# Attention and a mish MLP on one core: the copy of the softmax factors for GpSimd moves behind VectorE's own three tiles

## The chip, the cores and the metric

The kernel runs on one core of a Trainium2 chip. The metric is the device time of the core in microseconds (us), given as the median of several executions. Before the change it is 480.37 us (three runs, 480.23 to 481.23).

The engines are named as in the profile: PE is TensorE (PEld its weight loads), DVE is VectorE, ACT is ScalarE, POOL is GpSimd, SP is SyncE, which here only issues DMAs.

## The reference

The program has two parts. The first is attention for 8 batches of 12 heads, 448 tokens, 64 channels, with a softmax whose denominator has one term more than usual:

```python
scores = scale * np.matmul(q, k.transpose(0, 1, 3, 2))
m = np.max(scores, axis=-1, keepdims=True)
e = np.exp(scores - m)
attn = e / (np.sum(e, axis=-1, keepdims=True) + np.exp(-m) + 1e-09)
return np.matmul(attn, v).astype(np.float32)
```

Its output, as 3584 rows of 768, goes through an MLP with a mish-like activation:

```python
h = x @ w_in                      # 768 -> 2048
sp = np.where(h > 20.0, h, np.log1p(np.exp(np.minimum(h, 20.0))))
g = h * np.tanh(sp)
return (g @ w_out).astype(np.float32)   # 2048 -> 768
```

All inputs and the output are float32; the kernel computes its matmuls in bfloat16.

## The kernel before

**Tiling.** Heads are worked on in pairs: 8 batches of 6 pairs are 48 pairs, numbered p = 0 to 47. A pair has 2 x 448 = 896 query rows, which are 7 tiles of 128 rows (NTILE = 7). For each tile the scores against all 448 keys lie in PSUM, and the exponentials go to a buffer `en` in SBUF (128 rows, 4 groups of keys, 7 tiles, 112 keys of a group). There are four `en` buffers, used in turn.

**One pair.** The pair's q and k are loaded by SP (`load_pair`, L132), cast to bfloat16 on GpSimd (`cast_pair`, L175 and L176, v in `cast_v`, L162), transposed on TensorE (L193) and copied out of PSUM (`evac_qk`, L212 to L235). `scores` makes the score matmuls in four steps (L266 to L289) and a maximum on DVE (L293); `exps` makes the exponentials and their sums on ACT (L306), and one more exponential for the added term of the denominator (L313). `denominators` adds the terms and takes the reciprocal on DVE (`rden`, L319 and L323). `normalise` multiplies each of the seven tiles of `en` by its row's factor. Then `en` must be turned, so that keys lie on the partitions: by a DMA transpose from SP (L345), or tile by tile on TensorE (`turn_on_pe`, L356, seven transposes to a group of keys, copied out of PSUM by DVE in L360). The turned tile `eT` is multiplied with v on TensorE (`av_pair`, L382), and the result is copied to `xT` (L391).

**Stages.** The first six pairs, those of batch 0, form the head: attention alone, pair after pair, four steps to a pair, since no MLP work exists yet. After the scores of pair p have begun, the pair before it is normalised. From pair 6 on the pairs come in units of three: in a unit the attention of a batch is interleaved with the MLP's two matmuls of earlier batches (`mm1_mish`, L406, its activation in L412; `mm2_part`, L472). The first matmul of the MLP starts at 63.40 us.

**Order of the work.** The order is written out by hand: the kernel is recorded under a manual schedule, and each engine carries out its instructions in the order in which the Python code issues them. The framework only adds the waits between engines. Each engine and each DMA queue is thus a line in which work stands behind what was issued before it. On GpSimd the casts of a later pair stand behind the tiles that it normalises; on SP the loads of later pairs stand behind the DMA transposes.

**Who normalises.** In the head, for the pairs 0 to 5, `normalise` is called with `shared=BY_POOL`, and BY_POOL is 4 (L564 and L573): GpSimd takes the tiles 0 to 3, DVE the tiles 4 to 6. In the later units, two pairs of three are done by DVE alone (L635 and L644), and one by GpSimd alone (`on_pool=True`, L646). Whenever GpSimd takes part, DVE first copies the seven factors per row from `rden` to a tile of their own, `rden2` (L331), which GpSimd's instructions read (L339); DVE's read `rden` (L341).

**How the pairs of the head are turned.** BY_PE (L518) names the pairs 2, 4, 5, 6 and 7 as those turned on TensorE; the pairs 0, 1 and 3 of the head go by DMA transpose. TURN_HEAD (L524) places the four groups of pair 2 in steps 2 and 3 of pair 3 and steps 0 and 1 of pair 4, and the first two groups of pair 4 in steps 2 and 3 of pair 5. AV_HEAD (L528) places the AV products of the pairs 0, 2 and 1 in the pairs 3 and 4. A group of L356 reads its seven tiles in order, so tiles of GpSimd's come first; each of the seven weight loads of a pair's first group waits for its own tile.

Of the kernel before, what the change touches and what calls it, by code (L numbers as in the profile page):

```python
# [9 lines left out]
FP32 = mybir.dt.float32  # L10
BF16 = mybir.dt.bfloat16
AF = mybir.ActivationFunctionType
ALU = mybir.AluOpType
# [6 lines left out]
def kernel(  # L20
# [9 lines left out]
    nc = tc.nc  # L30
# [6 lines left out]
    SP_ = S // NT  # L37
# [3 lines left out]
    NTILE = 2 * S // 128  # L41
# [11 lines left out]
    def pool(name, bufs, space=None):  # L53
        if space is None:
            return ctx.enter_context(tc.tile_pool(name=name, bufs=bufs))
        return ctx.enter_context(tc.tile_pool(name=name, bufs=bufs, space=space))
# [6 lines left out]
    st_pool = pool("st", 5)  # L63
# [261 lines left out]
    def normalise(p, dma=True, on_pool=False, shared=0):  # L325
        st = att[p]
        en = st["en"]
        if on_pool or shared:

            st["rden2"] = st_pool.tile([128, NTILE], FP32, tag="rden2", name="rden2")  # L330
            nc.vector.tensor_copy(out=st["rden2"], in_=st["rden"])  # L331
        for i in range(NTILE):
            pool_does = on_pool or i < shared
            args = dict(
                out=en[:, :, i, 0:SP_], in0=en[:, :, i, 0:SP_],
                scalar1=st["rden2" if pool_does else "rden"][:, i : i + 1],
            )
            if pool_does:
                nc.gpsimd.tensor_scalar(scalar2=1.0, op0=ALU.mult, op1=ALU.mult, **args)  # L339
            else:  # L340
                nc.vector.tensor_scalar(scalar2=None, op0=ALU.mult, **args)  # L341
        eT = eT_pool.tile([128, NT, 2 * S], BF16, tag="eT", name="eT")
        st["eT"] = eT
        if dma:
            nc.sync.dma_start_transpose(  # L345
                out=eT.rearrange("c j (i q) -> c (j i) q", q=128),
                in_=en.rearrange("q j i c -> q (j i c)"),
            )
# [199 lines left out]
    for p in range(HEAD):  # L548
        for s in range(STEPS):
            if s == 1 and p == 0:  # L550
                transpose_pair(p + 2)
            exps(p * STEPS + s)
            if p == 0 and s == 0:
                evac_qk(1, act=True)
            if s == 1:
                evac_qk(p + 2, act=True)
            flush_late()
            scores_ahead(HEAD * STEPS + 3)
            if s == (2 if p == HEAD - 1 else 0):
                load_pair(p + 4)  # L560
            if s == 0:
                if p:
                    denominators(att[p - 1])
                    normalise(p - 1, dma=p - 1 not in BY_PE, shared=BY_POOL)  # L564
                    transpose_pair(p + 2)
                cast_pair(p + 3)
                load_w(W_HEAD.get(p, 0))
            for part in TURN_HEAD.get((p, s), []):
                turn_on_pe(*part)
            if (p, s) in AV_HEAD:  # L570
                av_pair(AV_HEAD[p, s], act=True)
    denominators(att[HEAD - 1])
    normalise(HEAD - 1, dma=HEAD - 1 not in BY_PE, shared=BY_POOL)  # L573

    for u in range(UNITS_PER_B, N_UNITS + 2 * UNITS_PER_B):
# [50 lines left out]
        for f in range(FF_U):  # L626
            if moe:
                mm1_mish(b, w * FF_U + f)
            if u == UNITS_PER_B and f in (2, 6):
                load_w(1)  # L630
            if not attn:
                continue
            if f == 0:
                denominators(att[p0]["whole"])
                normalise(todo[0], dma=todo[0] not in BY_PE)  # L635
            if f in (1, 3, 5):
                transpose_pair(nxt + f // 2, bank=f // 2 % 2)
                evac_qk(nxt + f // 2)
            if nxt < DIAG_FROM and f in (4, 6):
                scores_ahead(nxt * STEPS + f // 2 - 1)  # L640
            if f == FF_U - 1:
                scores_ahead(min(nxt * STEPS + 3, N_PAIRS * STEPS))
            if f == 3:
                normalise(todo[1], dma=todo[1] not in BY_PE)  # L644
            if f == 4:
                normalise(todo[2], dma=todo[2] not in BY_PE, on_pool=True)  # L646
# [37 lines left out]
```

## Time and profile before

| what | value |
|---|---|
| median of three runs | 480.37 us (480.23 to 481.23) |
| the profiled execution: time | 479.95 us |
| the profiled execution: span from first to last instruction | 478.0 us |
| TensorE busy | 443.1 us (93%) |
| ACT busy | 350.0 us (73%) |
| DVE busy | 339.1 us (71%) |
| GpSimd busy | 181.1 us (38%) |
| copies of factors (L331) | 20, about 0.165 us each |
| DVE tiles (L341) | 214, median 0.330 us |
| GpSimd tiles (L339) | 122, median 0.641 us |

The profiled execution is one execution; its own time stands beside the span, and sums are made against it. A line of a group names the source line, the engine, the operation, output and input with their shapes, the count, then the busy time, the mean duration in ns, and the idle time of the engine just before with what ended it. A line of a timeline names the start, the duration of the whole merged group, the engine and the line. Instructions of DVE and ACT overlap a little at their ends, so that start to start is less than the duration. The chain that ended last lists, in order of time, the pieces of work in which each released the next.

### The profile page before, as it was taken

The numbers are of one execution on the slowest core, as the hardware profiler recorded it, in microseconds if no ns is written. First come the engines' busy times: TensorE is split into PE (matmuls) and PEld (weight loads), VectorE is DVE, ScalarE is ACT, GpSimd is POOL, SyncE is SP. The second block draws the span as 40 slices with busy tenths as digits, with TensorE's granted clock in tenths as the row PEclk, the third lists the DMA queues.
The fourth block names the chain that finished last, engine by engine and source line by source line (L and its number), as shares of the span: only waits on it lengthen the run. The fifth ranks groups of instructions, "written<-read, shape, count | busy, mean of one in ns | idle before, by whom it ended". The sixth has DMA issues, their size and how long they took to land.

```text
span 478.0 us, 8924 instructions
## 1 busy us (share of the span) xinstructions
PE 443.1 (93%) x3064; PEld 248.6 (52%) x3064; DVE 339.1 (71%) x680; ACT 350.0 (73%) x919; POOL 181.1 (38%) x315
## 2 busy tenths in 40 slices
PE   4565888898999999999999999999999999999997
PEld 2233544454655555555555555556555555556565
DVE  4888987968787886878687878788787869420021
ACT  5979678878787888979787878888897978412300
POOL 4877809255514334353535242433535340300000
PEclk9998798899999999999999999999999999999999
DMA  8999969999999989899999999899989595870113
GB/s 228 220 233 220 235 100 234 162 187 238 207 217 276 206 212 219 213 203 246 193 250 182 225 167 228 211 207 234 201 233 212 156 178 127 135 164 24 43 28 105
DMA packets 202381, 90.37 MB, mean 189 GB/s; under 512 B 159072, under 2 KB 198880, under 8 KB 202336
## 3 DMA queue, kind: packets, MB, share of 16 engines
q1 hardware_dynamic: 194848, 83.51, 81.3%
q0 software_dynamic: 7488, 6.29, 8.6%
q8 instruction: 24, 0.39, 0.3%
q14 instruction: 21, 0.17, 0.1%
HBM read 45.61 MB, written 11.01 MB: 118 GB/s over the span
## 4 chain that ended last, share of the span: by engine, by line
PE 76%; ACT 10%; DVE 9%; issue 2%; DMA 1%; POOL 0%; SPq 0%; DVEq 0%; ACTq 0%; POOLq 0%
PE mo L472 26%; PE mo L406 25%; ACT en L306 9%; PE sc L382 6%; DVE negm L293 6%; PE sc L266 5%; PE sc L406 4%; PE sc L193 3%; PE sc L272 2%; PE mo L356 1%; PE mo L382 1%; DVE en L341 1%; PE sc L280 1%; DVE eT L360 1%; DMA k_f<-in_k_dram 1%
## 5 line engine op out<-in xcount | busy, mean ns | idle before, releaser
L306 ACT ACTIVATE en<-sc,negm 128x448 bf16<-128x448 f32 x336 | 209.6, 637 | 26.4 <-DVE xT L391 10.4
L293 DVE TENSOR_REDUCE negm<-sc 128x2 f32<-128x896 f32 x192 | 180.7, 968 | 55.8 <-PE sc L275 26.0
L472 PE MATMUL mo<-w_out_sb,gT 128*128 128x384 bf16 (+1 forms) x912 | 142.3, 301 | 0.0
L406 PE MATMUL mo<-xT,w_in_sb 128*128 128x448 bf16 x672 | 137.7, 353 | 0.6 <-DVE xT L391 0.6
L412 ACT ACTIVATE gT<-mo 128x448 bf16<-128x448 f32 x112 | 61.3, 547 | 68.2 <-PE mo L406 68.1
L472 PEld LDWEIGHTS <-gT 128*128 128x128 bf16 x912 | 84.1, 98 | 48.2 <-issue 5.7
L339 POOL TENSOR_SCALAR en<-en,rden 128x448 bf16<-128x448 bf16 x122 | 76.4, 646 | 80.7 <-DVE rden L331 76.9
L406 PEld LDWEIGHTS <-w_in_sb 128*128 128x128 bf16 x768 | 72.9, 98 | 64.0 <-issue 3.0
L306 ACT ACTIVATION_READ_ACCUMULATOR en<-sc,negm 128x1 f32 x336 | 69.3, 206 | 0.0
L175 POOL CAST q_bf<-q_f 112x512 bf16<-112x512 f32 x47 | 29.0, 617 | 98.4 <-DMA q_f<-in_q_dram 98.0
L341 DVE TENSOR_SCALAR en<-en,rden 128x448 bf16<-128x448 bf16 x214 | 58.6, 345 | 0.9
L459 DVE COPY o_sb<-mo 128x384 f32<-128x384 f32 (+1 forms) x65 | 32.2, 495 | 35.1 <-PE mo L472 34.8
L266 PE MATMUL sc<-kT,qd 128*128 128x448 bf16 x168 | 47.7, 354 | 0.3 <-ACT en L306 0.2
L272 PE MATMUL sc<-kT,qd 64*128 64x448 bf16 x72 | 25.1, 411 | 12.7 <-ACT en L306 11.1
L382 PE MATMUL sc<-eT,v_bf 112*64 112x448 bf16 x288 | 34.1, 357 | 1.9 <-ACT en L306 1.7
L162 POOL CAST v_bf<-v_f 112x512 bf16<-112x512 f32 x48 | 29.5, 616 | 9.7 <-DMA v_f<-in_v_dram 8.8
L382 PEld LDWEIGHTS <-v_bf 112*64 112x64 bf16 x384 | 21.0, 112 | 22.8 <-issue 13.6
L176 POOL CAST k_bf<-k_f 112x512 bf16<-112x512 f32 x47 | 28.9, 616 | 7.5 <-DMA k_f<-in_k_dram 7.0
L227 DVE TENSOR_SCALAR qd<-sc 64x448 bf16<-64x448 bf16 x48 | 18.7, 389 | 11.9 <-PE sc L193 11.2
L266 PEld LDWEIGHTS <-qd 128*128 128x128 bf16 x168 | 16.3, 97 | 18.0 <-issue 9.2
L275 PE MATMUL sc<-kT,qd 64*128 64x448 bf16 x72 | 25.4, 415 | 0.0
L472 PE MATMUL mo<-w_out_sb,mid 128*128 128x384 bf16 x128 | 24.9, 326 | 0.0
(57 smaller groups left out, 340.1 us busy)
## 6 DMA issues: line engine op xcount, KB each, us to landing
q_f<-in_q_dram SPq DMA_DIRECT2D x48, 224.0 KB, 5.1
k_f<-in_k_dram SPq DMA_DIRECT2D x48, 224.0 KB, 5.4
v_f<-in_v_dram SPq DMA_DIRECT2D x48, 224.0 KB, 5.7
w_in_sb<-in_moe_w_in_dram POOLq DMA_DIRECT2D x12, 256.0 KB, 6.1
w_out_sb<-in_moe_w_out_dram POOLq DMA_DIRECT2D x8, 384.0 KB, 7.6
out_dram<-o_sb SPq DMA_DIRECT2D x7, 336.0 KB, 3.3
out_dram<-o_sb SPq DMA_DIRECT2D x8, 288.0 KB, 4.6
out_dram<-o_sb SPq DMA_DIRECT2D x8, 240.0 KB, 2.9
```

The source lines that it names most:

```text
L162: nc.gpsimd.tensor_copy(out=casted[p][2], in_=loaded.pop(p)[2])
L266: nc.tensor.matmul(sc[:, bk, 0:S], lhsT=qT[:, i].rearrange("d h r -> d (h r)"), rhs=kT, start=True, stop=True,)
L272: nc.tensor.matmul(sc[:, 0, 0:S], lhsT=qT[0:64, qa : qa + 128], rhs=kA, start=True, stop=True)
L293: nc.vector.tensor_reduce(out=negm, in_=sc[:, 0 : len(cols), 0:S], axis=AX.X, op=ALU.max, negate=True)
L306: nc.scalar.activation(out=st["en"][:, :, c, 0:SP_], in_=sc[:, bk, 0:S].rearrange("q (j c) -> q j c", j=NT), func=AF.Exp, bias=st["negm"][ ...
L339: nc.gpsimd.tensor_scalar(scalar2=1.0, op0=ALU.mult, op1=ALU.mult, **args)
L341: nc.vector.tensor_scalar(scalar2=None, op0=ALU.mult, **args)
L382: nc.tensor.matmul(av[h * 64 : (h + 1) * 64, 0:S], lhsT=v_bf[:, h, j * D : (j + 1) * D], rhs=e_h, start=(j == 0), stop=(j == NT - 1),)
L406: nc.tensor.matmul(h_ps[:, 0:S], lhsT=w_in_sb[:, dm, ff * 128 : (ff + 1) * 128], rhs=xT[b][:, dm, :], start=(dm == 0), stop=(dm == DM_T - 1),)
L412: nc.scalar.activation(out=gT[b][:, ff, :], in_=h_ps[:, 0:S], func=AF.Mish)
L459: nc.vector.tensor_copy(out=o_sb[:, cols], in_=st["o"][:, 0:n_cols])
L472: nc.tensor.matmul(st["o"][:, 0:n_cols], lhsT=src[:, ff, c0 : c0 + 128], rhs=w_out_sb[:, ff, cols], start=(ff == 0), stop=(ff == FF_T - 1),)
```

## The change

In `normalise` the loop over all seven tiles is split. DVE's tiles, from `n_pool` to 6, now come first; after them, if GpSimd has tiles, DVE copies the factors, and GpSimd's tiles follow. Where GpSimd does a whole pair, DVE has no tile of that pair, so its order does not change; where DVE does a whole pair there is no copy. The order on DVE thus changes in the pairs 0 to 5 alone: three tiles and then the copy, in place of the copy and then three tiles. The order on the other engines and on the DMA queues is the same. In the changed file the lines from there on have numbers larger by two (L356 becomes L358, L382 becomes L384, and so on); DVE's tiles become L335, the copy L339, GpSimd's tiles L341.

```diff
-        if on_pool or shared:
-
-            st["rden2"] = st_pool.tile([128, NTILE], FP32, tag="rden2", name="rden2")
-            nc.vector.tensor_copy(out=st["rden2"], in_=st["rden"])
-        for i in range(NTILE):
-            pool_does = on_pool or i < shared
-            args = dict(
-                out=en[:, :, i, 0:SP_], in0=en[:, :, i, 0:SP_],
-                scalar1=st["rden2" if pool_does else "rden"][:, i : i + 1],
-            )
-            if pool_does:
-                nc.gpsimd.tensor_scalar(scalar2=1.0, op0=ALU.mult, op1=ALU.mult, **args)
-            else:
-                nc.vector.tensor_scalar(scalar2=None, op0=ALU.mult, **args)
+        n_pool = NTILE if on_pool else shared
+
+        def scaled(i, rden):
+            tile_i = en[:, :, i, 0:SP_]
+            return dict(out=tile_i, in0=tile_i, scalar1=rden[:, i : i + 1])
+
+        for i in range(n_pool, NTILE):
+            nc.vector.tensor_scalar(scalar2=None, op0=ALU.mult, **scaled(i, st["rden"]))
+        if n_pool:
+
+            rden2 = st_pool.tile([128, NTILE], FP32, tag="rden2", name="rden2")
+            nc.vector.tensor_copy(out=rden2, in_=st["rden"])
+            for i in range(n_pool):
+                nc.gpsimd.tensor_scalar(
+                    scalar2=1.0, op0=ALU.mult, op1=ALU.mult, **scaled(i, rden2)
+                )
```

## The prediction

> **What bounds the kernel now.** I read the page's busy times and slices first, then the chain that ended last, then the timeline around the six pairs that the change touches, then which waits the late work would meet.
>
> The page's busy times, the slices of the granted clock, and the two groups at stake:
>
> ```profile
> PE 443.1 (93%) x3064; PEld 248.6 (52%) x3064; DVE 339.1 (71%) x680; ACT 350.0 (73%) x919; POOL 181.1 (38%) x315
> ...
> PEclk9998798899999999999999999999999999999999
> ...
> L339 POOL TENSOR_SCALAR en<-en,rden 128x448 bf16<-128x448 bf16 x122 | 76.4, 646 | 80.7 <-DVE rden L331 76.9
> ...
> L341 DVE TENSOR_SCALAR en<-en,rden 128x448 bf16<-128x448 bf16 x214 | 58.6, 345 | 0.9
> ```
>
> From 63 us on TensorE hardly stops, so whatever the first 63 us (the head) lose reaches the end in full. The change touches only pairs 0 to 5, normalised between 17 and 54 us. The chain of waits there, around pair 2:
>
> ```profile
> 28.54 0.21 DVE rden L323
> 28.75 0.02 issue
> 28.77 0.17 DVE rden L331
> ...
> 30.90 0.53 PE sc L272
> 31.42 0.03 PE sc L275
> 31.45 0.98 PE mo L356 x7
> 32.44 0.48 PE sc L272
> ```
>
> TensorE turns pair 2 (L356) on the path itself; four of its seven tiles are GpSimd's. The timeline of the normalising, pair 0 (17 us) and pair 2 (28 us):
>
> ```profile
> 17.28 0.17 DVE L331 COPY rden<-rden 128x7 f32<-128x7 f32 x1
> 17.36 0.82 DVE L341 TENSOR_SCALAR en<-en,rden 128x448 bf16<-128x448 bf16 x3
> 18.10 1.08 DVE L293 TENSOR_REDUCE negm<-sc 128x2 f32<-128x896 f32 x1
> ...
> 28.85 1.13 DVE L341 TENSOR_SCALAR en<-en,rden 128x448 bf16<-128x448 bf16 x3
> 29.90 1.07 DVE L293 TENSOR_REDUCE negm<-sc 128x2 f32<-128x896 f32 x1
> ...
> 29.11 2.60 POOL L339 TENSOR_SCALAR en<-en,rden 128x448 bf16<-128x448 bf16 x4 [1.47 <-DVE rden L331]
> 31.66 0.61 POOL L175 CAST q_bf<-q_f 112x512 bf16<-112x512 f32 x1
> ```
>
> Three DVE tiles take 0.82 us in pair 0, where GpSimd's first tile took 0.96 beside them, and 1.13 in pair 2, where the third DVE tile alone took 0.64 and GpSimd's first 0.74. So one of the two engines pays some 0.3 us where they overlap.
>
> Last, busy time and granted clock in stretches of 3.41 us (columns: stretch, length, then busy time of PE, PEld, DVE, ACT, POOL, then the clock):
>
> ```profile
> 30.88:34.29 3.41, 3.39 (x22) 2.16 (x23) 2.82 (x5) 1.91 (x7) 3.21 (x6) 1.00 1.14 255
> 34.29:37.70 3.41, 2.25 (x28) 1.41 (x25) 2.68 (x9) 2.69 (x8) 1.00 (x2) 1.00 0.97 210
> 41.12:44.53 3.41, 1.47 (x16) 0.80 (x13) 2.49 (x8) 3.41 (x12) 1.40 (x2) 1.00 1.20 216
> 47.94:51.36 3.42, 2.75 (x20) 1.82 (x20) 3.28 (x10) 2.41 (x8) 1.69 (x4) 0.50 1.08 264
> 51.36:54.77 3.41, 3.41 (x20) 1.43 (x19) 3.41 (x6) 2.06 (x6) 3.41 (x7) 0.50 1.13 247
> 78.67:82.08 3.41, 3.29 (x25) 2.25 (x22) 3.25 (x5) 3.36 (x12) 3.41 (x7) 0.50 1.04 234
> ```
>
> The clock changed at about 44.53 (down), 54.77 (up), 78.67 (down) and 82.08 (up): steps of 3, 7 and 1 times 3.41 us. Before 34.3 us the column says 1.00, yet the same matmul took 0.53 us at 30.90 and 0.35 at 36.83, so it rose at 34.29 too, on the same grid. It rose after stretches with TensorE busy 3.39, 3.41 and 3.29 us, and not after 2.75.
>
> **The change part by part.** Nothing is added or removed. In six pairs a 7-wide copy (0.17 us) moves on DVE behind three tiles. SP, ACT and GpSimd keep their order.
>
> *GpSimd starts later.* DVE's tiles start every 0.247 us where nothing disturbs them ((18.10 - 17.36) / 3), so the copy starts 0.74 later. GpSimd follows a copy's start by 0.34 to 0.37, as now. Its four tiles lose their contended start: the last three of pair 2 start every 0.61, so four take 2.44 instead of the 2.55 from 29.11 to 31.66. In pair 2: copy 29.51, first tile 29.85, last tile done near 32.30, not 31.71: 0.59 later. For pairs 1, 3, 4, 5 about the same, for pair 0 only 0.4, as its first tile takes 0.6 instead of 0.96.
>
> *DVE is free earlier.* Next operation at 29.51 + 0.08 = 29.59 instead of 29.90: 0.31 sooner in pairs 1 to 5, nothing in pair 0. In pairs 0 to 3 this is worth nothing: ACT's exps run without a gap over it (no idle between 28.64 and 32.8), and they set the pace.
>
> *Pair 2.* TensorE's weight loads of L356 follow at 0.1 us; the fourth was held until 31.76, 0.05 after GpSimd's last tile. There is no slack, so the whole 0.59 is a stall: the next scores, transposes, and the AV of pair 0 whose result ACT awaits (idle 2.21 us before 35.01) slip by it. Price 0.59; bounds 0.45 (the delayed copy with GpSimd regaining all of 0.3) and 0.74 (regaining nothing).
>
> *Pair 4.* L356 at 46.30; its fourth load came at about 46.62 with GpSimd done at 46.44. Now GpSimd is done 0.63 later, the load at 47.12: TensorE slips 0.5. DVE, busy until 47.48 anyway, slips 0.37. It then wins 0.31 back in pair 5, where it is the path (the eT copy at 50.63 releases L356 at 51.29). Net +0.06; bounds -0.31 and +0.5.
>
> *Pairs 0, 1, 3 and 5.* The DMA transposes of 0, 1 and 3 follow GpSimd's last tile or queue behind each other on SP: 0.4 to 0.6 later. They land in 8.3 to 9.6 us, so by about 30.1, 37.0 and, with both delays, 50.7; their readers run at 33.8, 40.4 and 60.3. The loads behind them on SP move as much as the casts that read them. Pair 5's turning starts at 54.76, GpSimd is done at about 53.4. The casts queued behind GpSimd's tiles finish k for the next pair at 21.98 and 27.73, 0.14 ahead of their loads into TensorE (22.12, 27.87): covered, narrowly. Weight loads issued by GpSimd at 55.74 and 58.18 feed matmuls after 91 us.
>
> *The clock.* With 0.59 us of stall the first stretch holds 3.39 - 0.59 = 2.80 us of work: nearest to the row with 2.75, after which the clock stayed down. Then it rises at 37.70, and the rest of the AV (0.66 warm), L286 (0.30), the transposes of the next pair (0.51) run cold: TensorE +1.5, of which ACT's queued exps hide about 1; ACT's qd starts near 37.8 instead of 36.66, 1.14 late, so 0.55 over the stall. Bounds: 0, if 2.80 is enough, and 1.6, if two later stretches are missed as well (51.36 and its next, 0.55 each). I take 0.55. [...]
>
> *Sum:* 0.59 + 0.06 + 0.55 = 1.20 on the profiled execution's 479.95 (span 478.0 and 1.95 around it): 481.15. That execution lies 0.42 under the median of 480.37; if runs of before differ in when their clock rises, some already pay part of the 0.55, and from the median I add 0.65 and about 0.2: 481.2. Both agree; the forecast is 481.2 us, +0.17%.
>
> **The rivals.**
> *Faster: DVE was the path.* If DVE's 0.31 counted in all of pairs 1 to 5, 1.55 us would go: 478.8. For it: the chain shows DVE's tiles at 28.94, and pair 5 does gain. Against: ACT has no gap there, and pair 2's stall stands in any case. It decides if GpSimd's last tile comes no later than now, which needs its tiles in 0.46 us each; the quickest here follow each other at 0.58. [...]
> *The clock is missed more widely.* Two later stretches too: 479.95 + 0.65 + 1.6 = 482.2. For it: any shift moves gaps across a fixed grid. Against: a gap may as well move out.
> *No clock effect:* 0.65 alone, 480.6 to 481.0.
> *Casts late.* If GpSimd needs 0.15 more per pair, k is late in two pairs and passes to ACT's qd, up to 0.4 each: 482.0.
> *The delay is hidden* (the order of DVE does change, but the fourth load has slack I don't see): 480.0 to 480.4.
>
> **How the numbers follow.** About 0.2% (1 us) is what a measurement can tell from no change. Forecast with one missed stretch 0.40 (480.8 to 481.7, half on each side of +0.2%, 481.33); no clock effect 0.20; clock missed more widely 0.20; casts late 0.06; hidden 0.05; faster 0.09. Slower 0.20 + 0.20 + 0.06 = 0.46, same 0.20 + 0.20 + 0.05 = 0.45, faster 0.09. The range reaches from 480.1 to 482.5: it leaves out the faster case and the ends of the others.
>
> **What would show it.** GpSimd's tiles after a gap-free 0.74 us of DVE tiles; four tiles in 2.44; a gap of about 0.6 inside the first L356 group of pair 2; L382 behind it at cold durations (eight in 1.7 instead of 1.18); ACT idle 2.8 or more before pair 0's xT; first MoE matmul about 1.2 after 63.40. Wrong if that group has no gap, or if the head ends no later.

## The result, and the profile after

The changed kernel takes 482.03 us, the median of twelve runs (480.89 to 483.26), beside 480.24 us for the kernel before (twelve runs, 479.11 to 482.86). The ratio is 1.0036, 95% interval 1.002 to 1.0052: slower by 0.96 to 2.5 us. A second measurement gave 481.89 beside 480.64 us, ratio 1.001, interval 0.9988 to 1.0031, which by itself does not exclude that nothing changed. (The ratios here and below are those on record; they can differ from the quotient of the two medians, which is 1.0026 in this case.) Together: slower, by somewhere near 0.2 to 0.3%, and the two intervals share 1.002 to 1.0031.

The profiled execution of the changed kernel took 482.24 us, with a span of 480.4 us; before it was 479.95 and 478.0. Its page, the lines that answer to those shown of before:

```profile
PE 445.3 (93%) x3064; PEld 249.5 (52%) x3064; DVE 337.4 (70%) x680; ACT 349.6 (73%) x919; POOL 179.4 (37%) x315
...
L341 POOL TENSOR_SCALAR en<-en,rden 128x448 bf16<-128x448 bf16 x122 | 75.3, 635 | 83.2 <-DVE rden L339 74.9
...
L335 DVE TENSOR_SCALAR en<-en,rden 128x448 bf16<-128x448 bf16 x214 | 57.1, 338 | 1.1
```

DVE is busy 1.7 us less than before (339.1 to 337.4) and GpSimd 1.7 us less (181.1 to 179.4): the two no longer meet at the start of a pair's normalising. TensorE is busy 2.2 us more (443.1 to 445.3) with the same 3064 matmuls. The engines that gained are not those that set the end.

Pair 2 in the timeline of the changed kernel, first DVE and GpSimd:

```profile
28.68 0.83 DVE L335 TENSOR_SCALAR en<-en,rden 128x448 bf16<-128x448 bf16 x3
29.42 0.16 DVE L339 COPY rden<-rden 128x7 f32<-128x7 f32 x1
29.50 1.08 DVE L293 TENSOR_REDUCE negm<-sc 128x2 f32<-128x896 f32 x1
...
29.75 2.48 POOL L341 TENSOR_SCALAR en<-en,rden 128x448 bf16<-128x448 bf16 x4 [1.46 <-DVE rden L339]
32.18 0.61 POOL L175 CAST q_bf<-q_f 112x512 bf16<-112x512 f32 x1
```

DVE's three tiles take 0.83 us instead of 1.13, and DVE goes on with the maxima at 29.50 instead of 29.90. GpSimd starts at 29.75 instead of 29.11 and its four tiles take 2.48 instead of 2.60. Then TensorE, which turns the pair, before and after:

```profile
31.39 1.05 PE L356 MATMUL mo<-ident,en 128*112 128x128 bf16 x7
...
33.78 1.18 PE L382 MATMUL mo<-eT,v_bf 112*64 112x448 bf16 x8
```

```profile
30.79 0.53 PE L272 MATMUL sc<-kT,qd 64*128 64x448 bf16 x1 [1.87 <-ACT en L306]
...
31.28 0.75 PE L358 MATMUL mo<-ident,en 128*112 128x128 bf16 x3
32.29 0.68 PE L358 MATMUL mo<-ident,en 128*112 128x128 bf16 x4 [0.26 <-POOL en L341]
...
34.30 1.70 PE L384 MATMUL mo<-eT,v_bf 112*64 112x448 bf16 x8
```

Before, the seven transposes ran without a gap from 31.39. Now the group breaks after three of them, and the fourth starts at 32.29, when GpSimd's fourth tile is done. The product behind it takes 1.70 us instead of 1.18, because the clock had not risen yet. The chain of waits around the same place answers to the chain shown of before (start, duration, engine, tile, line; some pieces left out). It is from a second profile of the changed kernel, as the chain of the first is not followed back so far:

```profile
28.81 0.32 DVE en L335
...
29.64 0.09 DVE rden L339
...
29.89 0.94 POOL en L341 x2
...
31.11 0.43 POOL en L341
...
31.73 0.65 POOL en L341
...
32.42 0.67 PE mo L358 x4
```

Before, the chain went from DVE's tiles over a maximum and ACT's exponentials to TensorE's scores. It now goes over the copy and all four tiles of GpSimd: GpSimd has become the path.

The stretches of 3.41 us in which the clock should rise (columns as shown before: stretch, length, then busy time of PE, PEld, DVE, ACT, POOL, then the clock):

```profile
31.64:35.06 3.42, 3.16 (x21) 1.91 (x22) 2.96 (x4) 1.08 (x4) 2.96 (x5) 1.00 1.23 293
35.06:38.47 3.41, 3.41 (x25) 1.88 (x21) 1.90 (x9) 2.42 (x7) 0.00 (x0) 1.00 1.24 167
```

After the first, with TensorE busy 92% of it, the clock stayed down; after the second, at 38.47, it rose (the same matmul takes 0.55 us at 38.06 and 0.35 at 39.97). The column of the clock says 1.00 throughout, as it did before; the durations show the change.

Pair 4 breaks in the same way, again after three tiles:

```profile
47.33 0.57 PE L358 MATMUL mo<-ident,en 128*112 128x128 bf16 x3
48.15 0.67 PE L358 MATMUL mo<-ident,en 128*112 128x128 bf16 x4 [0.25 <-POOL en L341]
```

At the end of the head the first matmul of the MLP, before and after:

```profile
63.40 1.41 PE L406 MATMUL mo<-xT,w_in_sb 128*128 128x448 bf16 x6 [0.58 <-DVE xT L391]
```

```profile
64.44 1.41 PE L408 MATMUL mo<-xT,w_in_sb 128*128 128x448 bf16 x6 [0.15 <-DVE xT L393]
```

It starts 1.04 us later.

### The profile page after: what moved, and what is told of

The parts are those of the page before. It is cut to its first block, busy times and chain, and to the rows that moved or that the text cites. A ratio compares the mean times of both kernels' runs of the same rounds, so it can differ in the third digit from the quotient of the medians.

```text
span 480.4 us, 8925 instructions
## 1 busy us (share of the span) xinstructions
PE 445.3 (93%) x3064; PEld 249.5 (52%) x3064; DVE 337.4 (70%) x680; ACT 349.6 (73%) x919; POOL 179.4 (37%) x315
## 4 chain that ended last, share of the span: by engine, by line
PE 73%; DVE 8%; ACT 5%; DMA 2%; issue 1%; POOL 0%; DVEq 0%
PE mo L408 26%; PE mo L474 25%; PE sc L384 6%; ACT en L306 5%; PE sc L266 5%; DVE negm L293 5%; PE sc L408 4%; PE sc L193 3%; PE sc L272 2%; DMA eT<-en 2%; DVE eT L362 1%; PE mo L384 1%; DVE en L335 1%; PE sc L280 1%; PE mo L358 1%
## 5 line engine op out<-in xcount | busy, mean ns | idle before, releaser
L341 POOL TENSOR_SCALAR en<-en,rden 128x448 bf16<-128x448 bf16 x122 | 75.3, 635 | 83.2 <-DVE rden L339 74.9
L175 POOL CAST q_bf<-q_f 112x512 bf16<-112x512 f32 x47 | 28.8, 612 | 98.2 <-DMA q_f<-in_q_dram 97.8
L335 DVE TENSOR_SCALAR en<-en,rden 128x448 bf16<-128x448 bf16 x214 | 57.1, 338 | 1.1
L461 DVE COPY o_sb<-mo 128x384 f32<-128x384 f32 (+1 forms) x65 | 32.2, 495 | 35.1 <-PE mo L474 34.8
L384 PE MATMUL sc<-eT,v_bf 112*64 112x448 bf16 x288 | 34.1, 356 | 3.0 <-ACT en L306 2.0
L384 PEld LDWEIGHTS <-v_bf 112*64 112x64 bf16 x384 | 20.9, 112 | 23.9 <-issue 13.9
```

Of the source, the lines that this page charges most:

```text
L335: nc.vector.tensor_scalar(scalar2=None, op0=ALU.mult, **scaled(i, st["rden"]))
L384: nc.tensor.matmul(av[h * 64 : (h + 1) * 64, 0:S], lhsT=v_bf[:, h, j * D : (j + 1) * D], rhs=e_h, start=(j == 0), stop=(j == NT - 1),)
L461: nc.vector.tensor_copy(out=o_sb[:, cols], in_=st["o"][:, 0:n_cols])
```

## The experiments

Most of the kernels here are the changed kernel with the choice between old and new order made per pair, by this edit; each experiment then names its condition:

```diff
-        for i in range(n_pool, NTILE):
-            nc.vector.tensor_scalar(scalar2=None, op0=ALU.mult, **scaled(i, st["rden"]))
+        def by_dve():
+            for i in range(n_pool, NTILE):
+                nc.vector.tensor_scalar(scalar2=None, op0=ALU.mult, **scaled(i, st["rden"]))
+        if tiles_first:
+            by_dve()
         if n_pool:
...
+            if not tiles_first:
+                by_dve()
```

One table serves them all but the kernel without the copy. Every matmul of a kernel was matched with the same matmul in the first profile of before; the slip is its start less that one's start, in us. The profiles differ by -0.27 to +0.17 us at 30.5 us, ahead of pair 2's turning, and each kernel's own difference there is taken off. "Clock" is the time at which the duration of like matmuls drops for the first time after pair 2.

| kernel | slip at 32, pair 2's first group | clock rises | at 37 | at 47, after pair 4 | at 51, after pair 5 | first MLP matmul | at 100 | at 145 | end |
|---|---|---|---|---|---|---|---|---|---|
| before, first profile | 0 | 34.3 | 0 | 0 | 0 | 0 | 0 | 0 | 0 |
| before again | 0 | 34.3 | 0.12 | 1.43 | 1.32 | 1.49 | 0.37 | 1.43 | 1.33 |
| changed | 0.63 | 38.5 | 1.15 | 1.63 | 1.14 | 1.15 | 1.15 | 2.06 | 2.41 |
| changed again | 0.62 | 38.1 | 1.14 | 1.62 | 1.14 | 1.16 | 0.44 | 2.02 | 2.45 |
| pair 2 undone | 0 | 34.1 | 0 | 0.48 | 0 | -0.01 | -0.01 | 0.41 | 0.69 |
| pair 2 alone | 0.62 | 37.1 | 1.15 | 1.12 | 1.11 | 2.32 | 1.30 | 1.50 | 1.37 |
| pairs 0, 1, 3, 5 | 0 | 36.8 | 0.52 | 0.33 | -0.05 | -0.04 | -0.77 | 0.48 | 0.35 |
| pairs 0, 1, 3, 5 again | 0 | 37.5 | 0.52 | 0.61 | 0.13 | 0.13 | -0.78 | -0.68 | -0.75 |
| pair 5 alone | 0 | 37.1 | 0.53 | 0.20 | 0.02 | 0.01 | -0.73 | -0.51 | -0.65 |
| DVE's tiles turned first | 0.30 | 38.0 | 0.82 | 0.98 | 0.50 | 0.49 | 0.49 | 0.41 | 0.56 |
| stall filled | 0.66 | 34.3 | 0.35 | 0.84 | 0.35 | 0.35 | -0.47 | -0.07 | 0.22 |
| pair 2, delay doubled | 1.36 | 38.8 | 1.88 | 1.56 | 1.74 | 2.43 | 1.31 | 3.49 | 3.69 |
| pairs 0, 1, 3, 5, DVE's tiles turned first | -0.06 | 35.1 | 0.32 | 0.30 | -0.07 | -0.08 | -1.07 | 0.57 | 0.41 |

### Pair 2 undone, and pair 2 alone

The theory is that the new order costs time by pair 2 alone. The two kernels take it out and put it in by itself; the first line is the condition of pair 2 undone, the second that of pair 2 alone.

```diff
+        tiles_first = not (shared and p == 2)
```

```diff
+        tiles_first = not shared or p == 2
```

> The changed kernel, with pair 2 alone in the old order (copy, then DVE's tiles). Theory A (the loss is GpSimd's late last tile, for which TensorE stalls in the first turning of pair 2, and the clock that rises later for it): the first group of pair 2 has no gap, the first matmul of the MLP comes at 63.2 to 63.8 us, and the time is within 0.6 us of before, about +0.2. Rival B (the loss is spread: whatever stands behind GpSimd's tiles and on SP, in any of the six pairs, is late): five of six pairs are still changed, so 1.2 to 1.5 us of the 1.7 remain. Rival C (the loss is the wait for a DMA transpose at 138 us that the changed kernel's profile shows, and it comes from the transposes of pairs 0, 1 and 3 being late on SP): that wait of 0.8 us is still there.

> The kernel before, with the new order in pair 2 alone. Theory A: a gap of 0.2 to 0.3 us in TensorE inside the first group of pair 2, first MLP matmul near 64.3 us, +1.0 to +1.7 us in time. Rival B: a sixth of the loss, +0.3 us. Rival C: no wait at 138 us, so what is left is at most the 1.0 us of the head.

With pair 2 undone: 480.39 beside 480.58 us, ratio 0.9991 (0.9978 to 1.0003). With pair 2 alone: 480.88, ratio 1.0004 (0.9989 to 1.0019). In the table the stall in the first group (0.62) is there with pair 2 in the new order and gone without, exactly as with the whole change; so is the clock's 0.53 on top of it, though kernels further down pay that without a stall. Pair 2 undone also shows pair 4 and pair 5 by themselves: 0.48 lost at pair 4, 0.48 won back at pair 5, nothing left at the first MLP matmul. Of the times, the one with pair 2 undone contradicts rival B, which wanted 1.2 to 1.5 us more. The one with pair 2 alone missed its expectation: +0.30 us in the medians, an interval of about -0.5 to +0.9, where theory A said 1.0 to 1.7. Taken alone it would fit rival B, so here it is the traces that speak for theory A. The wait of rival C was there in both profiles, with 0.5 and 0.2 us; it is taken up below.

Pair 2 alone lost 1.2 us more between 51 and 64 us, where its clock stayed down for longer. The same group of transposes, in pair 2 alone and then in pair 2 undone (timelines; L286 took 0.58 us at 58.48, so at 64.65 the clock is up again):

```profile
58.99 0.99 PE L365 MATMUL mo<-ident,en 128*112 128x128 bf16 x7
...
64.65 0.37 PE L286 MATMUL sc<-kT,qd 64*64 64x448 bf16 x1
```

```profile
57.01 0.60 PE L365 MATMUL mo<-ident,en 128*112 128x128 bf16 x7
```

This is the rival "the clock is missed more widely", in one profile. The changed kernel itself did not show it.

### The change without the two pairs that TensorE turns early

If the loss comes from the pairs 2 and 4 and the gain from pair 5, the new order in the other pairs alone should be at least as quick as before.

```diff
+        tiles_first = not shared or p not in (2, 4)
```

> The new order in pairs 0, 1, 3 and 5, the old one in pairs 2 and 4, which TensorE turns while GpSimd still works on them. Theory A: no change, -0.3 to +0.3 us, first MLP matmul at 63.1 to 63.5 us. Rival B: four sixths of the loss, +1.1 us. Rival C: the wait at 138 us is there, +0.8 us.

> The kernel with the new order in pairs 0, 1, 3 and 5 once more, to tell its gain from chance. Theory: -0.3 to -0.5 us, so that with both measurements the mean gain lies between 0.3 and 0.8 us. Rival (the 1.0 us of the first measurement was chance): no gain, or a loss.

First measurement: 479.5 beside 480.58 us, ratio 0.9979 (0.9962 to 0.9995). Second: 479.86 beside 480.78, ratio 0.9989 (0.9968 to 1.001). Both medians gained more than was expected, 1.08 and 0.92 us, though the second interval still contains no change. No stall in pair 2, no slip at the first MLP matmul beyond 0.13. Both kernels paid the clock's 0.52 at 37 us without any stall, as their clock rose at 36.8 and 37.5.

### DVE's tiles turned first

If TensorE waits because it reads GpSimd's tiles first, it should wait less when it reads DVE's first and GpSimd's after.

```diff
-        for i in range(NTILE):
+        first = (*range(BY_POOL, NTILE), *range(BY_POOL)) if p in (2, 4) else range(NTILE)
+        for i in first:
```

> The changed kernel, but TensorE turns the tiles of pairs 2 and 4 in the order 4, 5, 6, 0, 1, 2, 3, so DVE's tiles, which are ready, come first and GpSimd's last tile is wanted 0.35 us later. Theory A: the gap of 0.26 us in the first group of pair 2 goes or falls under 0.1, pair 4's gap of 0.25 likewise, the loss falls to 0.3 to 0.9 us. Rival B and rival C: GpSimd, SP and the casts are as late as in the changed kernel, so the loss stays at 1.7 us.

480.58 beside 480.58 us, ratio 1.0005 (0.999 to 1.0021). The group of seven has no gap in the timeline of TensorE, but it is longer, 1.35 instead of 1.05 us, as it still ends on GpSimd's last tile:

```profile
31.16 1.35 PE L359 MATMUL mo<-ident,en 128*112 128x128 bf16 x7
```

The slip halves, from 0.63 to 0.30, and at the first MLP matmul it is 0.49 instead of 1.15. The time is that of before, with an interval of about -0.5 to +1.0 us.

### The stall filled

If the clock's part depends on how long TensorE is busy in a stretch of 3.41 us, as the prediction took it (a rise after 3.29 us and more, none after 2.75), work in place of the wait should save it. Here TensorE does five more transposes of a tile that it has already turned, into the same place, while it waits. They add work and change no value.

```diff
+            if (p, j, i) == (2, 0, 3):
+                for _ in range(5):
+                    nc.tensor.transpose(ps[0:SP_, 2, :], st["en"][:, j, 2, 0:SP_], ident)
```

> The changed kernel, but TensorE turns tile 2 of pair 2 five times more, between tiles 2 and 3 of the first group, into the same place, so that it works through the 0.3 to 0.6 us for which it would wait on GpSimd. The time of the wait is still lost (first MLP matmul about as late), but the stretch of 3.41 us stays busy. If the stall costs time through the clock as well, the clock rises within 3.4 us of 30.8 us plus its phase, as in the kernel before, and the loss falls from 1.7 to about 0.9 us. If the clock's rise depends on the phase alone, nothing changes: 1.0 to 1.7 us lost.

The timeline of TensorE in this kernel, the five in the middle line:

```profile
31.38 0.75 PE L361 MATMUL mo<-ident,en 128*112 128x128 bf16 x3
31.93 0.74 PE L360 MATMUL mo<-ident,en 128*112 128x128 bf16 x5
32.46 0.63 PE L361 MATMUL mo<-ident,en 128*112 128x128 bf16 x4
...
34.37 0.95 PE L387 MATMUL mo<-eT,v_bf 112*64 112x448 bf16 x8
```

The slip after the group is the same 0.66, but the clock rises at 34.3 and the product runs in 0.95 us instead of 1.70. Some of the stall is even won back: the slip at 37 us is 0.35, not 1.15. The time is 481.37 beside 480.64 us, ratio 1.0003 (0.998 to 1.0027), which decides nothing. This one profile alone can't say whether the fill or the phase of the grid raised the clock, since the clock of kernels without any stall also rises early or late (the table); the phases of all profiles, compared in the part on the prediction, speak for the fill.

### The delay doubled

A theory with a price should give it twice. The new order is in pair 2 alone, and DVE multiplies its three tiles a second time, by one, before it copies the factors: extra work of the same length.

```diff
+    unit = singles.tile([128, NTILE], FP32, tag="unit", name="unit")
+    nc.vector.memset(unit, 1.0)
...
+        tiles_first = not (shared and p in (0, 1, 3, 4, 5))
+        if tiles_first:
+            by_dve()
+        if shared and p == 2:
+            for i in range(n_pool, NTILE):
+                nc.vector.tensor_scalar(scalar2=None, op0=ALU.mult, **scaled(i, unit))
```

> The kernel before, with the new order in pair 2 alone, and there DVE multiplies its three tiles by one a second time ahead of the copy, so that GpSimd starts 0.74 us later still. Theory A (TensorE's slip is GpSimd's delay, one for one): the slip in the first group of pair 2 goes from 0.5 to 0.6 us to 1.2 to 1.35, the gap in TensorE's records from 0.26 to about 0.95; the time +1.2 to +2.2 us. Rival (the slip has another cause, and GpSimd's last tile is only near it): the slip stays at 0.6.

482.73 beside 480.78 us, ratio 1.0042 (1.0025 to 1.006). The timeline of TensorE, where each of three tiles is now waited for:

```profile
31.56 0.35 PE L370 MATMUL mo<-ident,en 128*112 128x128 bf16 x1
32.07 0.35 PE L370 MATMUL mo<-ident,en 128*112 128x128 bf16 x1 [0.16 <-POOL en L353]
32.68 0.35 PE L370 MATMUL mo<-ident,en 128*112 128x128 bf16 x1 [0.26 <-POOL en L353]
33.30 0.67 PE L370 MATMUL mo<-ident,en 128*112 128x128 bf16 x4 [0.26 <-POOL en L353]
```

The slip is 1.36, that is 0.74 more than with the plain order, and 0.74 us is what three DVE tiles take at 0.247. So the delay goes through one for one. The idle time in the records adds up to 0.68 us, less than the 0.95 expected of it.

### Pair 5 alone, and the best order

Pair 5's gain should stand by itself; and the two helpful edits together should be the quickest. First pair 5 alone, then the best order, which joins two edits shown above.

```diff
+        tiles_first = not shared or p == 5
```

```diff
+        tiles_first = not shared or p not in (2, 4)
...
+        first = (*range(BY_POOL, NTILE), *range(BY_POOL)) if p in (2, 4) else range(NTILE)
```

> The kernel before, with the new order in pair 5 alone, where DVE is the path and nothing waits for GpSimd's tiles. Theory (the only gain of the new order is DVE's 0.3 to 0.45 us in pair 5): as much as with the pairs 0, 1, 3 and 5 together, -0.3 to -0.5 us, seen as a step of TensorE's slip between 46 and 52 us in the profile. Rival (the earlier DVE helps in every pair that is not turned while GpSimd works): a quarter of the 1.0 us that the four pairs showed, -0.25 us in time and no step of its own.

> The new order in pairs 0, 1, 3 and 5, the old one in pairs 2 and 4, and TensorE turns the tiles of pairs 2 and 4 in the order 4, 5, 6, 0, 1, 2, 3. Theory: pair 5's gain of 0.3 to 0.45 us, and the wait of 0.1 us that the kernel before still has in pair 2's first group goes: 479.3 to 480.1, where before has 480.2 to 480.6; it should be the best of all, by little. Rival: the fourth weight load is not what holds TensorE; then it equals the kernel with the four pairs alone.

Pair 5 alone: 479.43 beside 480.78 us, ratio 0.9983 (0.9959 to 1.0006). DVE's timeline in it:

```profile
49.63 0.83 DVE L336 TENSOR_SCALAR en<-en,rden 128x448 bf16<-128x448 bf16 x3
50.37 0.17 DVE L344 COPY rden<-rden 128x7 f32<-128x7 f32 x1
50.45 0.61 DVE L369 COPY eT<-mo 112x896 bf16<-112x896 bf16 x1
```

The same place before, with TensorE, which waits on the copy of `eT`, in the last line:

```profile
49.51 0.17 DVE L331 COPY rden<-rden 128x7 f32<-128x7 f32 x1
49.59 1.13 DVE L341 TENSOR_SCALAR en<-en,rden 128x448 bf16<-128x448 bf16 x3
50.63 0.60 DVE L360 COPY eT<-mo 112x896 bf16<-112x896 bf16 x1
...
51.29 0.91 PE L356 MATMUL mo<-ident,en 128*112 128x128 bf16 x7 [0.67 <-DVE eT L360]
```

From the first of the pair's operations to the copy of `eT` it is 50.45 - 49.63 = 0.82 us; before, from the copy of the factors on, it was 50.63 - 49.51 = 1.12. The step in TensorE's slip is 0.18 us in pair 5 alone, less than the 0.3 to 0.45 expected. Over the whole table the slip falls by 0.18 to 0.49 between 47 and 51 us wherever pair 5 has the new order, and by no more than 0.11 where it has the old one. The best order together: 480.11 beside 480.78, ratio 0.9983 (0.9968 to 0.9997). It was expected to be the best of all and is not: turning DVE's tiles first adds nothing that shows when the pairs 2 and 4 keep the old order.

So the four measurements in which pair 5 has the new order and the pairs 2 and 4 the old one are quicker than before by 0.67 to 1.35 us in the medians, two of four with an interval below 1. They are the quickest kernels here. The profiles account for 0.2 to 0.5 us of it at most, by pair 5: at the first MLP matmul all four stand within 0.13 us of the first profile of before, as they had lost 0.32 to 0.53 to the clock at 37 us. Where the rest comes from is not shown, and much of it lies within the intervals.

### No copy at all

The copy looks dispensable: GpSimd can read `rden` itself. If it only delays GpSimd, the kernel without it should be quicker.

```diff
-            st["rden2"] = st_pool.tile([128, NTILE], FP32, tag="rden2", name="rden2")
-            nc.vector.tensor_copy(out=st["rden2"], in_=st["rden"])
...
-                scalar1=st["rden2" if pool_does else "rden"][:, i : i + 1],
+                scalar1=st["rden"][:, i : i + 1],
```

> The kernel before without any copy: GpSimd reads the factors where DVE wrote them, in all 20 pairs with its share. Copies of 0.17 us go and GpSimd starts about 0.24 us sooner, DVE 0.08. Theory A: in pair 2 the 0.1 us for which the fourth weight load still waits goes, in pair 5 DVE gains 0.08; in the units GpSimd has no deadline that is met late. So -0.1 to -0.4 us, hard to tell from none. If reading one tile from two engines costs (GpSimd's first tile longer than the 0.74 us of before), 0 to +0.5 us.

490.8 (four runs) beside 480.64 us, ratio 1.0191 (1.0149 to 1.0233): ten microseconds slower, far outside what was expected and by far the largest effect in this study. The page's two groups:

```profile
L340 DVE TENSOR_SCALAR en<-en,rden 128x448 bf16<-128x448 bf16 x214 | 98.2, 526 | 1.1
...
L338 POOL TENSOR_SCALAR en<-en,rden 128x448 bf16<-128x448 bf16 x122 | 77.6, 653 | 38.0 <-DVE rden L323 32.9
```

DVE's 214 tiles cost 98.2 us instead of 58.6; GpSimd's mean goes from 646 to 653 ns. A unit's normalising in the timeline of this kernel, and then the same place before:

```profile
95.75 1.81 DVE L340 TENSOR_SCALAR en<-en,rden 128x448 bf16<-128x448 bf16 x7
...
98.56 4.38 POOL L338 TENSOR_SCALAR en<-en,rden 128x448 bf16<-128x448 bf16 x7
...
100.05 4.21 DVE L340 TENSOR_SCALAR en<-en,rden 128x448 bf16<-128x448 bf16 x7
```

```profile
98.01 1.82 DVE L341 TENSOR_SCALAR en<-en,rden 128x448 bf16<-128x448 bf16 x7
...
100.11 4.34 POOL L339 TENSOR_SCALAR en<-en,rden 128x448 bf16<-128x448 bf16 x7 [4.61 <-DVE rden L331]
```

Before, the copy stands behind DVE's seven tiles in DVE's order, so GpSimd could not start until they were done: seven tiles in 1.82 us, and then GpSimd alone. Without it the two run side by side, a DVE tile takes 0.60 us (4.21 / 7) instead of 0.26, and DVE is late for what stands behind it: the time for which ACT waits for DVE's `xT` copies adds up to 16.2 us instead of 10.4. One rival was not run: the two engines now also read the same tile `rden`, and that could cost as well. Two rows speak for the overlap. In this same kernel DVE's seven tiles take 1.81 us at 95.75, where GpSimd does not normalise; and in the kernel before, with separate factor tiles, DVE's third tile of pair 2 took 0.64 us beside GpSimd's first.

### The two kernels once more

> The changed kernel once more, for a second profile. Chance theory (the wait of 0.85 us for a DMA transpose at 138 us depends on how long the first transpose of that unit takes to issue, 6.6 to 8.3 us in the profiles so far, whatever the order of the copies): that issue time comes out elsewhere and the wait with it; TensorE's gap in pair 2, about 0.26 us in the records, and 0.5 to 0.6 us of slip stay; the clock rises between 35.7 and 39.1 us. Rival (the late head causes the wait): it is there again with 0.7 to 1.0 us. Time: +1.0 to +1.9 us over before.

> The kernel before once more, for a second profile. Chance theory: the clock's first rise lies anywhere between 34.3 and 37.7 us, not at 34.3 as in the first profile, and if later than 35 us the first MLP matmul is up to 0.6 us later than 63.4; the wait at 138 us may show here too (0 to 1 us). Rival (both belong to the changed kernel): rise at 34.3, first MLP matmul at 63.4, no wait at 138.

The changed kernel: 481.89 us, span 480.5. The kernel before, one execution: 481.07, span 479.2, against 478.0 in its first profile. The changed kernel repeats the slips of its head to 0.01 us up to the first MLP matmul. The kernel before does not. Its clock rises at 34.3 us again, as the rival had it, but it waits 1.33 us at 41.65 us for the DMA transpose of pair 1, which landed 13.9 us after its issue (9.6 in the first profile), in the timeline and in the list of waits (columns: engine, tile and line, releaser; total, times, longest):

```profile
41.65 0.95 PE L382 MATMUL mo<-eT,v_bf 112*64 112x448 bf16 x8 [1.33 <-DMA eT<-en]
```

```profile
PE sc L382 <- DMA eT<-en: 1.0, 2, 0.8
```

The second line is from 128 to 142 us, where it waits 1.0 us in all for two other transposes, at 132 and at 138 us. The same place in the two profiles of the changed kernel:

```profile
PE sc L384 <- DMA eT<-en: 0.9, 1, 0.9
```

```profile
PE sc L384 <- DMA eT<-en: 1.5, 2, 0.9
```

In the first profile of before there is no wait there. So this wait of 0 to 1.5 us comes with either order, and a difference between two single profiles contains it. The wait at 138 us came back in the changed kernel with 0.86 us, which is what the rival of the late head asked for; that rival falls by other kernels. Those with the new order in pairs 0, 1, 3 and 5, whose head is not late, waited there 1.2 us in one profile (1.0 of it is put down to DVE in the list, but ended as the transpose landed) and not at all in the other, and the best order waited 1.6.

## Why the prediction was right, and what in it was not

**Forecast 481.2 us (+0.17%), measured +0.36% (0.2 to 0.52) and +0.1% (-0.12 to 0.31).** The sign and the range held: 482.03 and 481.89 lie in 480.1 to 482.5. The forecast lies inside the second interval and just under the first: in the medians it is 0.8 and 0.7 us too low.

**GpSimd starts 0.74 later and regains part.** Right. In the changed kernel the copy starts 0.74 after DVE's first tile (29.42 - 28.68), GpSimd's four tiles take 2.43 to the next operation (32.18 - 29.75; predicted 2.44), and DVE is free sooner.

**Pair 2: 0.59.** Right: 0.62 to 0.66 in the four profiles with the plain new order in pair 2 and TensorE's old one (the filled stall among them); zero in those without it; 1.36 with the delay doubled. That undoing moves it to zero and doubling adds 0.74 shows the cause.

**Pairs 4 and 5: +0.06 net.** Right: +0.48 and -0.48 with pair 2 undone, +0.48 and -0.49 in the changed kernel. The predicted terms were 0.37 and -0.31; both are larger, and cancel as forecast.

**Pairs 0 to 3 gain nothing by DVE.** Right. TensorE's scores at 30.79 (before: 30.90) start after a wait of 1.87 us for ACT's exponentials, and the 0.11 is within the -0.27 to +0.17 by which the profiles differ there. So no cast had been late by then.

**The clock: 0.55.** The size was right, 0.52 (1.15 - 0.63). The step took it from the stretches of the first profile of before, with a stall moved into one; that the grid might lie elsewhere in other runs entered the sum only as the "about 0.2" added to the median, an estimate of the author's that no run shows. What the runs show is a first rise at 34.1 to 38.8 us, and a price by it: three profiles with no stall at all (pairs 0, 1, 3, 5 twice, pair 5 alone) rose at 36.8 to 37.5 and paid 0.52, while both profiles of before and that of pair 2 undone rose at 34.1 to 34.3 and paid 0 to 0.12. With an unfilled stall all five rose at 37.1 or later.

The phases can be compared. TensorE works without a long break from its scores near 30.9 us on. In the first profile of before the granted clock changed at 44.53, 54.77, 78.67, 82.08, 88.91 and 92.32 us, in that of the changed kernel at 45.30, 52.13, 58.96, 62.37, 79.44, 82.85, 89.68 and 93.09: always a whole number of steps of 3.41 us apart, and in step with the rises at 34.29 and 38.47. Taking this step for the other profiles too, which is an estimate, and going back by it from each rise gives the start of the stretch that lies nearest to those scores. In nine profiles it began between 0.1 us before those scores and 0.9 after. The clock rose at its end in the five of them without an unfilled stall (before twice, pair 2 undone, the best order, the filled stall), and did not in the four with one (changed twice, DVE's tiles first, delay doubled). In the other four profiles the stretch began 0.2 to 0.9 us before the scores, so that it held idle time, and the clock stayed down with a stall or without. So the stall costs the 0.52 where the phase leaves the choice, in nine of these thirteen; in the rest a kernel pays it without a stall too.

**The sum for the head: 1.20.** Measured 1.15 and 1.16 at the first MLP matmul, against the first profile of before. So the step-by-step working held to 0.05 us, with some luck in the profile that it started from: the second profile of before was itself 1.49 later there, 1.33 of it by the wait for the transpose of pair 1. That the transposes land in 8.3 to 9.6 us, as the prediction had it, did not hold in general: 8.9 to 10.8 in the changed kernel, where no reader waited for them in the head, and 13.9 for that of pair 1 in the second profile of before.

**"Whatever the first 63 us lose reaches the end in full".** This step was too simple for single profiles. Between the first MLP matmul and 100 us the slips in the table change by 0 to -1.1 ("before again" from 1.49 to 0.37, "changed again" from 1.16 to 0.44), and from 100 to 145 us by -0.1 to +2.2 ("changed" +0.91, "before again" +1.06, "delay doubled" +2.18). The first comes from the clock between 80 and 92 us. The same sixteen products in the timeline of before and then in the second profile of the changed kernel:

```profile
88.57 2.91 PE L382 MATMUL mo<-eT,v_bf 112*64 112x448 bf16 x16
```

```profile
89.97 1.70 PE L384 MATMUL mo<-eT,v_bf 112*64 112x448 bf16 x16
```

In the first profile of before the clock falls (granted 0.50 from 88.91 to 92.32 us) and they take 2.91 us; in the other it stays up, by the durations, and they take 1.70. That is not a late head given back: nine of the thirteen profiles gain 0.7 to 1.1 us there, four of them with a head that was not late (-0.08 to +0.13 at the first MLP matmul). The second comes from the waits at 132 and 138 us for two DMA transposes, the first of which SP issues at about 122 us, the second behind it. In the thirteen profiles of the table SP took 6.6 to 7.6 us to issue the first one where the wait was 0 to 0.5 us, and 8.1 to 9.3 where it was 0.9 to 2.2 (first profile of before: 7.2 and 0, of the changed kernel: 8.1 and 0.9; TensorE's idle time before the two products; with the delay doubled, too, the list names ACT and DVE, but it ended as the transposes landed). Weight loads of GpSimd's queue are in flight then (before, the last two are issued at 118.3 and 119.0 us and land 7.3 to 9.1 us later); that they are the reason is not shown. The changed kernel's 2.41 us at the end of its first profile is 1.15 of the head, 0.91 at that transpose, and 0.35 later on, near 398 us. Only the first is shown to belong to the change. The waits for the transposes came with either order, and with heads that were late or not. The wait near 398 us, 0.30 to 0.32 us of TensorE's time, stands in all five profiles whose kernel has the new order in pair 4 (changed twice, pair 2 undone, DVE's tiles first, stall filled) and in none of the other eight, so it may belong to the change too; how is not shown. In the mean over many executions the sentence may well hold: the two medians of +1.79 and +1.25 us leave room for the head's 1.15 alone or for some tenths more.

**The rivals.** *Faster, DVE is the path:* fell as a whole, since the changed kernel is slower. But its mechanism is real in pair 5, and only there: 0.30 us of DVE's time, and the kernels with the new order in pair 5 and the old one in the pairs 2 and 4 were the quickest. The traces also show that GpSimd and DVE disturb each other: DVE's three tiles of pair 2 took 1.13 us beside GpSimd's first and 0.83 ahead of it. *Clock missed more widely:* not in the changed kernel, but in the profile of pair 2 alone. *No clock effect:* fell, in both profiles of the changed kernel. *Casts late* fell, as the scores at 30.79 came on time, and *hidden* fell by the gap in pair 2.

## What to carry to other kernels

When one engine both works on its own share and opens the gate for another engine's, ask whose result is read first: here the copy belongs ahead of the tiles in pairs that TensorE reads at once (it cost TensorE 0.62 and 0.48 us in the two such pairs), and behind them where DVE itself is waited for (0.3 us of DVE's time). An instruction that looks redundant may keep two engines apart; the kernel without this copy took 10 us more. And before a microsecond between two profiles is explained, a second profile of the same kernel shows how much of it is the kernel's own spread: here 0.9 of 2.4 us.

## What the runs showed of the hardware that was not expected

- Side by side, DVE paid nearly everything in the kernel without the copy. With GpSimd multiplying another buffer by factors from the same tile, a 128x448 bf16 tile on DVE took 0.60 us instead of 0.26; GpSimd's seven tiles took 4.38 us instead of 4.34, and the mean of all its 122 was 0.653 instead of 0.646. In the kernel before, where the two overlap only briefly in the head, one engine paid about 0.3 us once: DVE 1.13 us for three tiles instead of 0.82 (pair 2), or GpSimd 0.96 for its first tile instead of about 0.6 (pair 0).
- After a stretch with TensorE busy 3.16 of 3.42 us (92%) the clock did not rise (changed kernel, from 31.64 us); after one with 3.29 of 3.41 (96%) it did (before, from 78.67). That is no sharp limit: in the kernel with DVE's tiles turned first the stretch from 31.20 us had 3.30 of 3.41 by the records (its timeline marks no idle time of TensorE from 30.67 to 35.55), and the clock stayed down until 38.0.
- In the first profiles of the two kernels the clock changed on a grid of 3.41 us. Its first rise lay anywhere from 34.1 to 38.8 us in the thirteen profiles. Without a stall a kernel was 0 to 0.12 us late at 37 us where it rose by 34.3, and 0.52 to 0.53 where it rose at 36.8 to 37.5.
- The issue of a DMA transpose by SP took 4.3 us in the median of each of the first profiles of the two kernels (43 transposes), but 7.2 and 8.1 us there for the first transpose of the unit near 122 us, and 6.6 to 9.3 in all thirteen; GpSimd's weight loads are in flight then. In the four profiles of the two kernels the wait that followed was 0 to 1.5 us. In the head the transpose of pair 1 took 5.8 and 6.3 us to issue in the first profiles; in the second profile of before it landed 13.9 us after its issue (9.6 in the first), and TensorE waited 1.33 us.
